# Fused attention and soft mixture of experts: the second expert layer of the last four experts by column halves

## The chip, the cores and the metric

The kernel runs on one core of a Trainium2 chip, as one program. The metric is the device time of one execution in microseconds. A core has the engines TensorE (PE; its weight loads are listed as PEld), VectorE (DVE), ScalarE (ACT), GpSimd (POOL) and SyncE (SP), which issues nearly all DMA transfers here. Sixteen DMA engines move the data.

## The reference

Attention over q, k, v of 8 batches, 8 heads, 576 tokens and 64 elements a head keeps for each query only the keys whose score is within tau of the best. Its output, 4608 tokens by 512, is the input x of a soft mixture of 8 experts with 4 slots each:

```python
logits = x @ phi                                   # 4608 x 32
d = softmax(logits, axis=0); slot_input = d.T @ x  # 32 slots x 512
for e in range(8):                                 # 4 slots per expert
    h = np.maximum(slot_input[e] @ w1[e], 0.0)     # 512 -> 1024
    slot_out[e] = h @ w2[e]                        # 1024 -> 512
c = softmax(logits, axis=1)
out = c @ slot_out                                 # 4608 x 512, fp32
```

## The kernel before

Attention, the logits and the running slot inputs take the first 469 us; a planner's table orders their instructions. The change touches only what follows. There each engine runs its instructions in the order in which the code names them, and so do the transfers on SyncE's queue.

The weights come in 32 units of 1 MiB: 0 to 15 are w1, 16 to 31 are w2, numbered by group of four experts (`a` is 0 or 1), by half of the contracted axis (`K`) and by expert in the group (`g`). So units 24 to 27 are the first half of w2 of experts 4 to 7, and 28 to 31 (`LAST`) the second. A unit is a tile of 128 partitions by 2048 elements; for w2 it holds 4 rows (`j`) of 512 columns in each partition. Units 0 to 22 and half of unit 31 (`early`, its rows j = 2, 3) are loaded during attention, the others when the first layer (`stage1`) frees a tile. `load_unit` loads each of the units 28 to 31 in two parts: first rows j = 0, 1 of all four, then rows j = 2, 3 of units 28 to 30, with 4 KB in one piece from each partition. That is seven transfers of 512 KB.

The second layer (`stage2`) multiplies `hz`, the transposed hidden values masked by expert, with w2. Four experts run side by side in four groups of 32 rows of TensorE, and all steps but the last add into one PSUM bank `so`. The last step (rows j = 2, 3 of units 28 to 31) goes into two other banks `end`, one for each half of the 512 columns, and meanwhile ScalarE copies `so` to SBUF (L1706). `combine` adds the banks to that copy (L1648), sums the four groups with a matmul by `st4` (L1651), and makes `sh` of it (L1652, L1653), which holds each value as two parts for the faster matmul type float32r.

The output of batch b is `cT` of the batch (128 by 512) times `sh`: four matmuls of 128 tokens, each 512 columns wide, into four PSUM banks (L1671). ScalarE copies two of them to SBUF (L1673), VectorE two (L1675), and SyncE writes them (L1679), 1 MiB for a whole batch with 8 KB in one piece per partition. Batch 0 goes in jobs of 1, 1 and 2 of its four parts, batch 1 in jobs of 2 and 2; the first job is done by column halves (L1664). A ninth batch holds the 64 last tokens of all eight batches (L1681). `ct` makes the next batch's `cT`: GpSimd scales the coefficients, TensorE transposes them (L976), ScalarE casts (L1570), VectorE subtracts (L1571). It is called after each batch, and there are three `cT` buffers.

Of the kernel before, what the change touches and what calls it, by code (L numbers as in the profile page):

```python
# [10 lines left out]
F32 = mybir.dt.float32  # L11
F32R = mybir.dt.float32r
# [826 lines left out]
def softmax_attention_soft_moe(  # L839
# [17 lines left out]
    nc = tc.nc  # L857
# [84 lines left out]
    wslots = [wp.tile([128, 2048], F32, name=f"w{i}") for i in range(NPRE)]  # L942
    where = {}
    early = wp.tile([128, 2, 512], F32, name="early")

    def load_early():
        e, K = units[-1][1:]
# [2 lines left out]
    def load_unit(t):  # L950

        i = len(where)
        if i == n_units:
            return
        where[i] = t
        kind, e, K = units[i]
        if kind == 0:
            nc.sync.dma_start(t.rearrange("p (j f) -> p j f", j=2),
                              w1[e, K * 256:(K + 1) * 256, :].rearrange("(j p) f -> p j f", j=2))
            return  # L960
        src = lambda e: w2[e, K * 512:(K + 1) * 512, :].rearrange("(p j) f -> p j f", j=4)
        if i not in LAST:
            nc.sync.dma_start(t.rearrange("p (j f) -> p j f", j=4), src(e))
        for k, h in [(i, 0)] * (i in LAST) + [(k, 1) for k in LAST[:-1]] * (i == LAST[-1]):
            nc.sync.dma_start(where[k].rearrange("p (j f) -> p j f", j=4)[:, 2 * h:2 * h + 2],
                              src(units[k][1])[:, 2 * h:2 * h + 2])


    rows = [slice(0, 64), slice(64, 128)]
# [532 lines left out]
    order_all.enter_context(tc.manual_schedule())  # L1502
    ps_h = ctx.enter_context(tc.tile_pool(name="ps_h", bufs=1, space=PSUM, reuse_waits="tile"))
    ps_t = ctx.enter_context(tc.tile_pool(name="ps_t", bufs=3, space=PSUM, reuse_waits="tile"))
    st4 = tl.tile([128, 4, 32], F32, name="st4")
    for g in range(4):
        nc.gpsimd.tensor_copy(st4[:, g, :], st1)
    neg = tl.tile([128, 1], F32, name="neg")
    for g in range(4):
        nc.gpsimd.memset(neg[g * 32:(g + 1) * 32], -1.0 if g % 2 else 0.0)  # L1510
# [5 lines left out]
    def ttile(name):  # L1516
        return ps_t.tile([128, 512], F32, tag="t", name=name)
# [22 lines left out]
    def ct():  # L1540


        if len(cTs) == len(blocks):
            return
        while len(c4s) < min(len(cTs) + 2, len(blocks)):
            c4s.append(c_block(*blocks[len(c4s)]))
        k = blocks[len(cTs)][1]
        c4 = c4s[len(cTs)]
        n = 128 * k
        t = tl.tile([128, SM], F32R, tag="cT", name=f"cT{len(cTs)}", bufs=3)  # L1550
        if len(cTs) < 2:
            w = two(f"ct{len(cTs)}", "h00" if cTs else "h01")
            for i in range(k):
                split(w, i, c4[:, i].rearrange("p g s -> p (g s)"))
            tv = t.rearrange("p (i g q) -> p i g q", i=4, g=2)
            for g in range(2):
                wv = w[g][:, 0:256].rearrange("p (i q) -> p i q", i=4)
                nc.scalar.copy(tv[:, :, g], wv)
                nc.vector.tensor_tensor(
                    out=tv[64:128, :, g], in0=wv[64:128], in1=tv[64:128, :, g].bitcast(F32), op=ALU.subtract)  # L1560
            cTs.append(t)
            return
        w = ttile(f"ct{len(cTs)}")
        for i in range(k):
            tr(w[:, i * 128:(i + 1) * 128], c4[:, i].rearrange("p g s -> p (g s)"))
        tv, wv = t[:, 0:n], w[:, 0:n]
        if len(cTs) == B:
            tv = t.rearrange("p (c r b) -> p b r c", c=4, b=B)
            wv = w.rearrange("p (b r c) -> p b r c", c=4, b=B)
        nc.scalar.copy(tv, wv)  # L1570
        nc.vector.tensor_tensor(out=tv[64:128], in0=wv[64:128], in1=tv[64:128].bitcast(F32), op=ALU.subtract)  # L1571
        cTs.append(t)
# [29 lines left out]
                    op=ALU.mult,  # L1602
                )

    def stage2(a, K, h):
        w = range(n_units // 2 + (a * 2 + K) * 4, n_units // 2 + (a * 2 + K) * 4 + 4)
        t = [where[i].rearrange("p (j f) -> p j f", j=4) for i in w]

        if a == NG - 1 and K == 1 and h == 1:
            for n, g in enumerate((3, 0, 1, 2)):  # L1610
                for q, dst in enumerate(end):
                    x = slice(q * DM // 2, (q + 1) * DM // 2)
                    for j in (2, 3):
                        m = (n + q) % 2 * 2 + j - 2
                        nc.tensor.matmul(
                            dst[m * 32:(m + 1) * 32, 0:DM // 2], hz[a][:, K * 4 + j, g * 32:(g + 1) * 32],
                            t[g][:, j, x] if g < 3 else early[:, j - 2, x], start=n < 2, stop=n > 1,
                            tile_position=(0, 32 * m), skip_group_check=True)
            return
        for j in (2 * h, 2 * h + 1):  # L1620
            for g in range(4):
                nc.tensor.matmul(
                    so[g * 32:(g + 1) * 32, :], hz[a][:, K * 4 + j, g * 32:(g + 1) * 32], t[g][:, j],
                    start=(a, K, j) == (0, 0, 0), stop=(a, K, j) == (NG - 1, 1, 1),
                    tile_position=(0, 32 * g), skip_group_check=True)
        if h:
            for i in w:
                load_unit(where[i])

    cnt = [-1]  # L1630

    def otile(name):
        cnt[0] += 1
        k = cnt[0] % 6
        return ps_h.tile([128, 512], F32, tag=("h01", "h10", "h11")[k // 2], name=name) if k % 2 else ttile(name)

    def through():

# [2 lines left out]
            last[id(where[i])] = (i, where[i])  # L1641
        return [t for i, t in sorted(last.values(), key=lambda x: x[0])]

    def combine():

        cols = [slice(n * DM // 2, (n + 1) * DM // 2) for n in range(2)]
        for q, w in zip(cols, end):
            nc.vector.tensor_tensor(out=so_sb[:, q], in0=w[:, 0:DM // 2], in1=so_sb[:, q], op=ALU.add)  # L1648
        for q, x in enumerate(cols):
            w = ttile(f"sr{q}")  # L1650
            nc.tensor.matmul(w[:, 0:DM // 2], st4.rearrange("p g s -> p (g s)"), so_sb[:, x], start=True, stop=True)  # L1651
            nc.scalar.copy(sh[:, x], w[:, 0:DM // 2])  # L1652
            nc.vector.scalar_tensor_tensor(  # L1653
                out=sh[:, x], in0=sh[:, x].bitcast(F32), scalar=neg, in1=w[:, 0:DM // 2], op0=ALU.mult, op1=ALU.add)
        free = through()

        jobs = [(0, 0, 1), (0, 1, 1), (0, 2, 2), (1, 0, 2), (1, 2, 2)] + [(b, 0, 4) for b in range(2, B + 1)]
        for n, (b, k, z) in enumerate(jobs):
            ot = free[b].rearrange("p (c d) -> p c d", c=4)[:, k:k + z]
            token = lambda c: slice(k + c, SM, 4) if b < B else slice(c * 128, c * 128 + 128)  # L1660
            for q, x in enumerate(cols if n == 0 else []):
                for c in range(z):
                    w = otile(f"o{n}_{c}_{q}")[:, 0:DM // 2]
                    nc.tensor.matmul(w, cTs[b][:, token(c)], sh[:, x], start=True, stop=True)  # L1664
                    if q:
                        nc.vector.tensor_copy(ot[:, c, x], w)
                    else:
                        nc.scalar.copy(ot[:, c, x], w)
            ws = [otile(f"o{n}_{c}") for c in range(z if n else 0)]
            for c in range(len(ws)):  # L1670
                nc.tensor.matmul(ws[c], cTs[b][:, token(c)], sh, start=True, stop=True)  # L1671
                if c % 2 == 0:
                    nc.scalar.copy(ot[:, c], ws[c])  # L1673
                else:
                    nc.vector.tensor_copy(ot[:, c], ws[c])  # L1675
            if k + z == 4:
                ct()
            if b < B:
                nc.sync.dma_start(out[b * S:b * S + SM].rearrange("(p c) d -> p c d", c=4)[:, k:k + z], ot)  # L1679
            else:  # L1680
                nc.sync.dma_start(out.rearrange("(b s) d -> b s d", s=S)[:, SM:S].rearrange(  # L1681
                    "b (r c) d -> r b (c d)", c=4), ot.rearrange("p c d -> p (c d)"))

    hp = [[ps_h.tile([128, 512], F32, tag=f"h{a}{n}", name=f"h{a}_{n}") for n in range(2)] for a in range(NG)]
    hid = [where[0][:, a * F:(a + 1) * F] for a in range(NG)]
# [4 lines left out]
    for a in range(NG):  # L1690
        for K in range(2):
            stage1(a, K, hp[a])
            if a == 0 and K == 0:
                for _, _, fn in csoft(slice(row(B - 1), NR)):
                    fn()
            if a and K == 0:
                hidden(a - 1)
        relu(a, hp[a])
    ct()
    ct()  # L1700
    end[:] = [ps_h.tile([128, 512], F32, tag=t, name=t + "e") for t in ("h00", "h11")]
    for a in range(NG):
        for K in range(2):
            for h in range(2):
                if a == NG - 1 and K == 1 and h == 1:
                    nc.scalar.copy(so_sb, so)  # L1706
                stage2(a, K, h)
            if a < NG - 1 and K == 0:
                hidden(a + 1)
    combine()  # L1710
    order_all.close()


# [45 lines left out]
```

## Time and profile before

| | us |
|---|---|
| runs, median of 3 (lowest to highest) | 535.15 (534.55 to 535.35) |
| span of the profiled execution, first to last instruction | 533.2 |
| first matmul of the first expert layer (L1579) | 468.85 |
| first instruction that waited for the last weights | 500.97 |
| issue of the first output transfer | 505.32 |
| issue of the last output transfer | 523.83 |

For the profiled execution no time is given but its span; the median is 1.95 us longer. Over the span TensorE is busy 97%, VectorE 88%, ScalarE 84%; 83.26 MB were moved, of which 9.44 MB are output. The stretch that the change touches is the last 50 us, so it has to be read by windows and by the timeline there, not from the shares of the whole span.

### The profile page before, as it was taken

Reading aid. Unit: us, or ns where it says so; the run is one execution under the profiler, and the core shown is the slowest. Engines: PE = TensorE matmul, PEld = TensorE weight load, DVE = VectorE, ACT = ScalarE, POOL = GpSimd, SP = SyncE. Lnnn points to the kernel's source line nnn. Section 1 sums busy time; section 2 is a strip of 40 time slices with the busy share of each in tenths; the row PEclk is TensorE's granted clock in tenths of the full one; section 3 lists DMA queues with packets and bytes.
Section 4 is the critical chain, followed back from the end, with each engine's and each line's share of the span. In section 5 each row is a group of like instructions: output and inputs, shape, how many; then the busy total and the mean of one; then the engine's idle time right before and its main releaser. Section 6 shows DMA issues by size and latency. Waiting matters only on the chain.

```text
span 533.2 us, 21792 instructions
## 1 busy us (share of the span) xinstructions
PE 514.7 (97%) x8877; PEld 403.5 (76%) x8877; DVE 467.3 (88%) x1311; ACT 447.4 (84%) x750; POOL 247.6 (46%) x444
## 2 busy tenths in 40 slices
PE   8999999999999999999999999999999999999881
PEld 5877888888878888888788888888788877643470
DVE  6999998999899998999899989999999999613282
ACT  3899998999899989998999989999899899612271
POOL 2475554556446454655356635554464546021030
PEclk9999999999999999999999999999999999999996
DMA  6333335333337314732953355353466315999398
GB/s 157 94 93 94 93 98 172 96 94 93 94 99 245 93 35 100 256 78 67 284 140 96 92 172 173 94 133 94 104 225 188 83 20 176 368 401 389 158 399 301
DMA packets 28868, 83.26 MB, mean 156 GB/s; under 512 B 4064, under 2 KB 12256, under 8 KB 26336
## 3 DMA queue, kind: packets, MB, share of 16 engines
q1 hardware_dynamic: 28448, 81.43, 49.5%
q8 instruction: 70, 1.15, 0.9%
q10 hardware_dynamic: 320, 0.44, 0.3%
q14 instruction: 30, 0.25, 0.2%
HBM read 72.42 MB, written 9.44 MB: 154 GB/s over the span
## 4 chain that ended last, share of the span: by engine, by line
PE 86%; DMA 4%; ACT 3%; DVE 3%; issue 2%; SPq 0%; DVEq 0%; ACTq 0%
PE ps L1068 24%; PE ps L1211 22%; PE ps L984 19%; PE ps L1234 4%; PE ps L1223 4%; PE ps L1073 3%; DMA w<-in_w 3%; PE ps L1268 2%; PE h L1579 2%; PE ps L1326 2%; PE ps L1376 2%; PE ps L1178 1%; ACT cT L1570 1%; DVE cT L1571 1%; PE ct L976 1%
## 5 line engine op out<-in xcount | busy, mean ns | idle before, releaser
L1080 DVE TENSOR_SCALAR_CACHE_REDUCE ss<-ps 128x576 f32<-128x576 f32 x288 | 208.3, 751 | 4.6 <-PE ps L1068 1.4
L1096 DVE SCALAR_TENSOR_TENSOR p<-ss,thr,p 128x576 f32<-128x576 f32 x256 | 203.6, 821 | 3.8 <-POOL thr L1093 1.6
L1093 POOL TENSOR_SCALAR thr<-nmx,pabs 128x1 f32<-128x1 f32 x288 | 136.1, 480 | 146.5 <-DVE ss L1080 143.2
L1090 ACT ACTIVATE p<-ss,nmx 128x576 f32<-128x576 f32 x256 | 188.6, 781 | 12.6 <-DVE ss L1080 11.6
L1068 PE MATMUL ps<-k,q 64*128 64x288 f32 x1024 | 154.9, 423 | 0.4
L1068 PEld LDWEIGHTS ps<-k,q 64*128 64x128 f32 x1024 | 87.5, 188 | 23.6 <-ACT pTa L989 5.1
L984 PEld LDWEIGHTS ps<-ident,p 64*128 64x128 f32 x2304 | 91.8, 138 | 17.2 <-DVE ss L1080 2.3
L984 PE MATMUL ps<-ident,p 64*128 64x64 f32 x2304 | 101.4, 223 | 0.2
L989 ACT COPY pTb<-ps 128x1024 f32<-128x1024 f32 (+1 forms) x96 | 83.8, 877 | 2.1 <-PE ps L984 0.7
L989 ACT COPY pTa<-ps 128x1024 f32<-128x1024 f32 x64 | 65.1, 1017 | 0.4 <-PE ps L984 0.2
L1211 PE MATMUL ps<-pTa,vv 128*64 128x128 f32 x992 | 61.0, 276 | 0.1
L1211 PE MATMUL ps<-pTb,vv 128*64 128x128 f32 x992 | 60.4, 274 | 0.0
L1211 PEld LDWEIGHTS ps<-pTa,vv 128*64 128x64 f32 x992 | 53.5, 137 | 5.5 <-issue 4.3
L1211 PEld LDWEIGHTS ps<-pTb,vv 128*64 128x64 f32 x992 | 53.6, 137 | 3.3 <-issue 2.8
L1263 POOL TENSOR_TENSOR x<-x,ri 128x512 f32<-128x512 f32 x31 | 37.2, 1201 | 10.3 <-ACT x L989 10.3
L1122 POOL TENSOR_SCALAR pL<-pL,ri 128x576 f32<-128x576 f32 x31 | 26.0, 840 | 15.2 <-DVE ri L1121 14.2
L1048 POOL TENSOR_SCALAR k<-k,flag 128x576 f32<-128x576 f32 x31 | 31.7, 1023 | 0.8 <-DMA k<-in_kT 0.4
L989 ACT COPY pTl<-ps 128x256 f32<-128x256 f32 x64 | 27.5, 429 | 3.3 <-PE ps L984 2.9
L1119 POOL TENSOR_SCALAR ri<-r 128x9 f32<-128x9 f32 x31 | 7.1, 229 | 45.4 <-DVE p L1096 44.6
L1223 PE MATMUL ps<-pTl,vv 64*64 64x128 f32 x496 | 26.5, 284 | 0.5 <-DVE ss L1080 0.5
L1249 ACT COPY xT<-ps 128x256 f32<-128x256 f32 x62 | 23.2, 374 | 4.4 <-PE ps L1211 2.6
L1532 POOL TENSOR_TENSOR w<-lall,crow 128x512 f32<-128x512 f32 x9 | 9.3, 1046 | 37.7 <-PE ct L976 24.4
(175 smaller groups left out, 609.0 us busy)
## 6 DMA issues: line engine op xcount, KB each, us to landing
w<-in_w SPq DMA_DIRECT2D x18, 1024.0 KB, 8.2
q<-in_qT SPq DMA_DIRECT2D x62, 288.0 KB, 4.5
vv<-in_vt SPq DMA_DIRECT2D x32, 320.0 KB, 4.8
host<-in_w SPq DMA_DIRECT2D x10, 1024.0 KB, 8.2
k<-in_kT SPq DMA_DIRECT2D x62, 144.0 KB, 4.2
out<-host SPq DMA_DIRECT2D x7, 1024.0 KB, 6.9
w<-in_w SPq DMA_DIRECT2D x7, 512.0 KB, 14.4
out<-host SPq DMA_DIRECT2D x2, 512.0 KB, 3.0
```

Of the source, the lines that this page charges most:

```text
L984: nc.tensor.transpose(out=s[:, g, c:c + 64], in_=ins[g], identity=ident[rows[g], rows[g]], tile_position=(64 * g, 0))
L989: G.add("ACT", 51 + 0.833 * n, nom, lambda: nc.scalar.copy(*io()), r, w)
L1048: sc = lambda e, kc=kc: lambda: e.tensor_scalar(out=kt.t[:, kc], in0=kt.t[:, kc], scalar1=flag8, **one)
L1068: nc.tensor.matmul(s.t[:, g, 0:HS], qt.t[rows[g], h, c * 128:(c + 1) * 128], kt.t[rows[g], h * HS:(h + 1) * HS], start=True, stop=True, ti ...
L1080: dve(678, t + OFF['mx'], [s], [ss, nmx], lambda s=s, ss=ss, nmx=nmx: nc.vector.tensor_scalar(out=ss.t.rearrange("p (a k) -> p a k", a=2), ...
L1090: G.add("ACT", 674, t + OFF['ex'], lambda sv=sv, nmx=nmx, view=view: nc.scalar.activation(view().rearrange("p (a k) -> p a k", a=2), sv(), ...
L1093: pool(250, t + OFF['th'], pre=75, fn=lambda nmx=nmx, thr=thr: nc.gpsimd.tensor_scalar(out=thr.t, in0=nmx.t, scalar1=1.0, scalar2=pabs, op ...
L1096: fn=lambda sv=sv, thr=thr, view=view, i=i: nc.vector.scalar_tensor_tensor(out=view().rearrange("p (a k) -> p a k", a=2), in0=sv(), scalar ...
L1122: pool(725, t + OFF['sc'], lambda: nc.gpsimd.tensor_scalar(out=pL.t[:, SL:SL + S], in0=pL.t[:, SL:SL + S], scalar1=ri.t[:, 8:9], **one), [ ...
L1211: nc.tensor.matmul(area(w, h, l)[rows[a]], vv.t[:, (h * 4 + kb) * 64:][:, 0:64], pT.t[:, h, kb, a * 128:(a + 1) * 128], tile_position=(0, ...
L1223: nc.tensor.matmul(area(ab[l], h, l)[rows[a]], vv.t[rows[h], SM + h * 64:][:, 0:64], pTl.t[rows[h], (l * 2 + a) * 128:][:, 0:128], tile_po ...
L1263: G.add("POOL", 1040, u + 6.8, own=f"new{j}" + group(b), r=[ri], w=[x[j]], fn=lambda: nc.gpsimd.tensor_tensor(out=wide(), in0=wide(), in1= ...
```

## The change

`load_unit` loads units 28 to 31 by column halves: columns 0 to 255 of all four rows j of units 28 to 30 and of rows 0, 1 of unit 31, then columns 256 to 511 of the same. That is eight transfers (six of 512 KB, two of 256 KB), in pieces of 1 KB.

The bank `so` now holds experts 0 to 3 alone. For experts 4 to 7 the whole second layer goes into the two banks `end`: `half(q, j)` multiplies one row j of units 24 to 27 for column half q, `half_unit(q, g)` all four rows of one of the units 28 to 31. `total(q)` does for one column half what the beginning of `combine` did for both. `out_half(b, q)` makes one column half of a batch's output: four matmuls of 256 columns into two banks, one copy each on ScalarE and VectorE, and one transfer of 512 KB in pieces of 1 KB. `out_whole(b)` is the old job for a whole batch.

The order is: column half 0 of experts 4 to 7, its total between the steps of half 1, then for each of the units 28 to 31 its second half followed by the output of column half 0 of batch 0, 1, 2 or 3 (and `ct` after the first two), then the total of half 1, the second column halves of batches 0 to 3 with a `ct` after each, and the other batches whole. `st4` moves from a tile of its own into the tile of unit 2, and `cT` gets a fourth buffer.

```diff
+    cols = [slice(n * DM // 2, (n + 1) * DM // 2) for n in range(2)]
...
-        for k, h in [(i, 0)] * (i in LAST) + [(k, 1) for k in LAST[:-1]] * (i == LAST[-1]):
-            nc.sync.dma_start(where[k].rearrange("p (j f) -> p j f", j=4)[:, 2 * h:2 * h + 2],
-                              src(units[k][1])[:, 2 * h:2 * h + 2])
+        for k, q in [(i, 0)] * (i in LAST) + [(k, 1) for k in LAST] * (i == LAST[-1]):
+            js = slice(0, 2 if k == LAST[-1] else 4)
+            nc.sync.dma_start(where[k].rearrange("p (j f) -> p j f", j=4)[:, js, cols[q]], src(units[k][1])[:, js, cols[q]])
...
-    st4 = tl.tile([128, 4, 32], F32, name="st4")
-    for g in range(4):
-        nc.gpsimd.tensor_copy(st4[:, g, :], st1)
...
-        t = tl.tile([128, SM], F32R, tag="cT", name=f"cT{len(cTs)}", bufs=3)
+        t = tl.tile([128, SM], F32R, tag="cT", name=f"cT{len(cTs)}", bufs=4)
...
+    def product(a, K, j, g, m, w, dst, q, **kw):
+        nc.tensor.matmul(dst[m * 32:(m + 1) * 32, 0:q.stop - q.start], hz[a][:, K * 4 + j, g * 32:(g + 1) * 32], w[:, q],
+                         tile_position=(0, 32 * m), skip_group_check=True, **kw)
+
+    def stage2(a, K):
+        t = w2_units(a, K)
+        for j in range(4):
             for g in range(4):
...
+                product(a, K, j, g, g, t[g][:, j], so, slice(0, DM), start=(K, j) == (0, 0), stop=(K, j) == (1, 3))
+
+    def half(q, j):
+
+        t = w2_units(NG - 1, 0)
+        for g in range(4):
+            product(NG - 1, 0, j, g, g, t[g][:, j], end[q], cols[q], start=j == 0, stop=False)
+
+    def half_unit(q, g):
+
+        t = w2_units(NG - 1, 1)[g]
+        for j in (2, 3, 0, 1):
+            w = early[:, j - 2] if g == 3 and j > 1 else t[:, j]
+            product(NG - 1, 1, j, g, j, w, end[q], cols[q], start=False, stop=g == 3)
+
+    def total(q):
+
+        x = cols[q]
+        nc.vector.tensor_tensor(out=so_sb[:, x], in0=end[q][:, 0:DM // 2], in1=so_sb[:, x], op=ALU.add)
+        w = ttile(f"sr{q}")
+        nc.tensor.matmul(w[:, 0:DM // 2], st4.rearrange("p g s -> p (g s)"), so_sb[:, x], start=True, stop=True)
+        nc.scalar.copy(sh[:, x], w[:, 0:DM // 2])
+        nc.vector.scalar_tensor_tensor(
+            out=sh[:, x], in0=sh[:, x].bitcast(F32), scalar=neg, in1=w[:, 0:DM // 2], op0=ALU.mult, op1=ALU.add)
...
+        return ps_h.tile([128, 512], F32, tag=("h01", "h10", "so")[k // 2], name=name) if k % 2 else ttile(name)
...
+    def out_half(b, q):
+
+        ot = through()[b].rearrange("p (c d) -> p c d", c=4)[:, :, cols[q]]
+        for k in range(2):
+            w = otile(f"o{b}_{q}_{k}").rearrange("p (c d) -> p c d", c=2)
+            for c in range(2):
+                nc.tensor.matmul(w[:, c], cTs[b][:, token(b, 2 * k + c)], sh[:, cols[q]], start=True, stop=True,
+                                 skip_group_check=True)
+            if k:
+                nc.vector.tensor_copy(ot[:, 2 * k:2 * k + 2], w)
             else:
...
+                nc.scalar.copy(ot[:, 2 * k:2 * k + 2], w)
+        nc.sync.dma_start(out[b * S:b * S + SM].rearrange("(p c) d -> p c d", c=4)[:, :, cols[q]], ot)
...
+    st4 = where[2][:, 3 * DM:3 * DM + 128].rearrange("p (g s) -> p g s", g=4)
+    for g in range(4):
+        nc.gpsimd.tensor_copy(st4[:, g, :], st1)
...
-    for a in range(NG):
-        for K in range(2):
-            for h in range(2):
-                if a == NG - 1 and K == 1 and h == 1:
-                    nc.scalar.copy(so_sb, so)
-                stage2(a, K, h)
-            if a < NG - 1 and K == 0:
-                hidden(a + 1)
-    combine()
+    for K in range(2):
+        stage2(0, K)
+        if K == 0:
+            hidden(1)
+    nc.scalar.copy(so_sb, so)
+    for j in range(4):
+        half(0, j)
+    for g in range(4):
+        half_unit(0, g)
+    for j in range(4):
+        half(1, j)
+        if j == 1:
+            total(0)
+    for g in range(4):
+        half_unit(1, g)
+        out_half(g, 0)
+        if g < 2:
+            ct()
+    total(1)
+    for b in range(4):
+        out_half(b, 1)
+        ct()
+    for b in range(4, B + 1):
+        out_whole(b)
```

## Rows read from the trace of the kernel before

**Rows 1.** Windows, us: busy PE, PEld, DVE, ACT, POOL; clock, DMA share, GB/s:
```profile
490.00:495.00 5.00, 5.00 (x52) 1.55 (x46) 0.00 (x0) 0.00 (x0) 0.00 (x0) 1.00 1.00 397
...
497.00:498.00 1.00, 0.83 (x9) 0.29 (x12) 0.00 (x0) 0.00 (x0) 0.00 (x0) 1.00 0.61 246
...
499.00:500.00 1.00, 1.00 (x17) 0.58 (x15) 0.00 (x0) 0.59 (x1) 0.00 (x0) 1.00 0.10 41
500.00:501.00 1.00, 0.47 (x13) 0.03 (x5) 0.00 (x0) 0.00 (x0) 0.00 (x0) 1.00 0.03 12
...
505.00:506.00 1.00, 1.00 (x8) 0.93 (x8) 0.61 (x2) 0.82 (x2) 0.00 (x0) 1.00 0.00 0
506.00:507.00 1.00, 1.00 (x5) 0.79 (x4) 0.56 (x2) 1.00 (x3) 0.81 (x1) 1.00 0.82 309
...
527.00:528.00 1.00, 0.00 (x0) 0.00 (x0) 0.00 (x0) 0.00 (x0) 0.00 (x0) 0.50 1.02 262
...
530.00:531.00 1.00, 0.00 (x0) 0.00 (x0) 0.00 (x0) 0.00 (x0) 0.00 (x0) 0.50 0.71 254
```

**Rows 2.** Timeline, 479 to 519 us (start, length, instruction, idle before it):
```profile
479.60 8.89 SPq L965 DMA_DIRECT2D w<-in_w  x7
...
497.23 0.16 PEld L1622 LDWEIGHTS so<-w,w 128*32 128x32 f32 x8 [1.07 <-DMA w<-in_w]
...
499.72 0.11 PEld L1615 LDWEIGHTS h00e<-w,w 128*32 128x32 f32 x2 [0.20 <-DMA w<-in_w]
...
500.97 0.11 PEld L1615 LDWEIGHTS h00e<-w,w 128*32 128x32 f32 x2 [1.01 <-DMA w<-in_w]
...
501.21 0.39 PE L1615 MATMUL h00e<-w,w 128*32 128x256 f32 x2
...
501.70 0.42 DVE L1648 TENSOR_TENSOR w<-h00e,w 128x256 f32<-128x256 f32 x1 [11.99 <-issue]
...
502.18 1.13 PE L1651 MATMUL sr<-w,st 128*128 128x256 f32 x4 [0.57 <-DVE w L1648]
...
503.94 0.85 PE L1664 MATMUL o<-sh,cT 128*128 128x256 f32 x2 [0.64 <-DVE sh L1653]
...
505.32 1.42 SPq L1679 DMA_DIRECT2D out<-w  x3
...
507.62 0.63 PE L976 MATMUL ct<-ident,w 128*128 128x128 f32 x4 [0.52 <-DVE cT L1571]
...
508.00 1.46 PE L1671 MATMUL o<-sh,cT 128*128 128x512 f32 x4
...
518.91 1.16 ACT L1570 CAST cT<-ct 128x512 fp32r<-128x512 f32 x1 [0.56 <-PE ct L976]
```

**Rows 3.** DMA view, 516 to 520 us, 8 KB output packets:
```profile
DMA packets 233, 1.65 MB, mean 414 GB/s; under 512 B 31, under 2 KB 31, under 8 KB 31
```

**Rows 4.** DMA view, 492 to 497 us, 4 KB weight packets:
```profile
DMA packets 565, 2.05 MB, mean 410 GB/s; under 512 B 64, under 2 KB 64, under 8 KB 565
```

**Rows 5.** DMA view, 506.2 to 506.8 us, 2 KB output packets:
```profile
DMA packets 110, 0.23 MB, mean 375 GB/s; under 512 B 0, under 2 KB 0, under 8 KB 110
```

**Rows 6.** DMA view, 258.8 to 259.2 us, 1152 B key packets:
```profile
DMA packets 127, 0.13 MB, mean 330 GB/s; under 512 B 15, under 2 KB 126, under 8 KB 127
```

**Rows 7.** Groups by line and shape, 478 to 533 us (busy us, mean ns, idle):
```profile
L1675 DVE COPY host<-o 128x512 f32<-128x512 f32 x16 | 10.2, 686 | 0.2
...
L1673 ACT COPY host<-o 128x512 f32<-128x512 f32 x16 | 8.7, 604 | 0.8 <-PE o L1671 0.8
...
L1571 DVE TENSOR_TENSOR cT<-ct,cT 64x512 fp32r<-64x512 f32 x7 | 5.3, 756 | 1.7 <-ACT cT L1570 1.1
L1570 ACT CAST cT<-ct 128x512 fp32r<-128x512 f32 x7 | 4.7, 673 | 3.4 <-PE ct L976 3.4
```

**Rows 8.** SyncE's issues of key loads and outputs, ns min/median/max:
```profile
L1032 SPq DMA_DIRECT2D k<-in_kT x62: 595/616/1390, 6.1 to 422.2; - x62
...
L1679 SPq DMA_DIRECT2D out<-host x8: 332/332/333, 508.3 to 522.6; - x8
```

More of the change, by code (lines that the diff above doesn't have):

```diff
@@ L1603, in hidden, with w2_units @@
                 )
-    def stage2(a, K, h):
+    def w2_units(a, K):
         w = range(n_units // 2 + (a * 2 + K) * 4, n_units // 2 + (a * 2 + K) * 4 + 4)
-        t = [where[i].rearrange("p (j f) -> p j f", j=4) for i in w]
-        if a == NG - 1 and K == 1 and h == 1:
[L1610 to L1620, printed above, removed]
-            for g in range(4):
[L1622 to L1628, printed above, removed]
@@ new lines, in w2_units @@
+        return [where[i].rearrange("p (j f) -> p j f", j=4) for i in w]
+    def product(a, K, j, g, m, w, dst, q, **kw):
[4 more added lines that the diff above has]
+        for j in range(4):
+            for g in range(4):
+                product(a, K, j, g, g, t[g][:, j], so, slice(0, DM), start=(K, j) == (0, 0), stop=(K, j) == (1, 3))
@@ L1634, in otile @@
         k = cnt[0] % 6
-        return ps_h.tile([128, 512], F32, tag=("h01", "h10", "h11")[k // 2], name=name) if k % 2 else ttile(name)
+        return ps_h.tile([128, 512], F32, tag=("h01", "h10", "so")[k // 2], name=name) if k % 2 else ttile(name)
     def through():
@@ L1642, in through @@
         return [t for i, t in sorted(last.values(), key=lambda x: x[0])]
[L1644 to L1679, printed above, removed]
-            else:
-                nc.sync.dma_start(out.rearrange("(b s) d -> b s d", s=S)[:, SM:S].rearrange(
-                    "b (r c) d -> r b (c d)", c=4), ot.rearrange("p c d -> p (c d)"))
@@ new lines, in token @@
+    def token(b, c):
+        return slice(c, SM, 4) if b < B else slice(c * 128, c * 128 + 128)
+    def out_half(b, q):
[7 more added lines that the diff above has]
+                nc.vector.tensor_copy(ot[:, 2 * k:2 * k + 2], w)
+            else:
+                nc.scalar.copy(ot[:, 2 * k:2 * k + 2], w)
+        nc.sync.dma_start(out[b * S:b * S + SM].rearrange("(p c) d -> p c d", c=4)[:, :, cols[q]], ot)
@@ new lines, in out_whole @@
+    def out_whole(b):
+        ot = through()[b].rearrange("p (c d) -> p c d", c=4)
+        ws = [otile(f"o{b}_{c}") for c in range(4)]
+        for c in range(4):
+            nc.tensor.matmul(ws[c], cTs[b][:, token(b, c)], sh, start=True, stop=True)
+            if c % 2 == 0:
+                nc.scalar.copy(ot[:, c], ws[c])
+            else:
+                nc.vector.tensor_copy(ot[:, c], ws[c])
+        ct()
+        if b < B:
+            nc.sync.dma_start(out[b * S:b * S + SM].rearrange("(p c) d -> p c d", c=4), ot)
+        else:
+            nc.sync.dma_start(out.rearrange("(b s) d -> b s d", s=S)[:, SM:S].rearrange(
+                "b (r c) d -> r b (c d)", c=4), ot.rearrange("p c d -> p (c d)"))
@@ L1701, in softmax_attention_soft_moe @@
     end[:] = [ps_h.tile([128, 512], F32, tag=t, name=t + "e") for t in ("h00", "h11")]
-    for a in range(NG):
-        for K in range(2):
-            for h in range(2):
-                if a == NG - 1 and K == 1 and h == 1:
-                    nc.scalar.copy(so_sb, so)
-                stage2(a, K, h)
-            if a < NG - 1 and K == 0:
-                hidden(a + 1)
-    combine()
+    for K in range(2):
[19 more added lines that the diff above has]
+        out_half(b, 1)
+        ct()
+    for b in range(4, B + 1):
+        out_whole(b)
     order_all.close()
```

## Prediction

> **What bounds the kernel now.** I read the windows first, then the timeline of the tail, then the DMA packets by size, then the durations of the few instructions that the change rearranges. Everything before 490 us is the same in both kernels, so the argument is about the last 43 us. In that stretch the DMA engines are the bound, and they are idle once. Their share is 1.00 while the last w2 units come in, falls from 497 on (0.61, then 0.10: most of the 16 engines are done and a few lag), is about zero from 500, and is 0.82 again in the microsecond from 506 [rows 1]. So the engines stand still for about 6 us, and partly for 3 us more. After that they are full until the last 1 MiB, which is slow (262 GB/s at 527) and ends near 531.1 [rows 1]. What fills the hole is one chain: the last weights release TensorE at 500.97, VectorE adds from 501.70, the sum over the expert groups starts at 502.18, the first output matmul at 503.94, and SyncE issues the first output transfer at 505.32 [rows 2]; its packets run from about 506.2, some 0.85 us after the issue. That output stream then sets the end. I check it: 16 packets of 2 KB per engine, 24 of 4 KB and 48 of 8 KB, at the prices below, are 1.4 + 3.8 + 15.2 = 20.4 us, so 526.6, and the slow last transfer takes 4.5 us more: 531.1, as the share is falling (0.71 from 530).
>
> **The price of a packet.** With the engines full the rate gives the time of one packet on one engine (16 times its size over the rate): 8 KB at 414 GB/s is 317 ns, 4 KB at 410 is 160, 2 KB at 375 is 87, and the 1152 B packets of the key loads at 330 are 56 [rows 3 to 6]. The change makes 1 KB packets, which no row shows. From below, the line through 8 and 4 KB gives 42 ns; from above, the 1152 B packets in proportion and the line through 4 and 2 KB give 50 and 51. I take 48, and keep 42 and the whole 56 as ends.
>
> The Trainium skill (DMA: Bandwidth & Descriptors, Specifications) puts the smallest transfer that still runs at line rate at 512 B. By that a 1 KB packet would cost an eighth of an 8 KB one, some 40 ns; the trace disagrees, since its packets of 1152 B reach 330 GB/s where 8 KB reach 414.
>
> **The change, part by part.**
>
> *Loads.* The same 3.5 MiB of units 28 to 31 come as 1 KB runs instead of 4 KB runs. The releases by weights stand 1.25 us apart on the latest engine (499.72 to 500.97), so the seven old transfers begin there at about 500.97 - 7 x 1.25 = 492.2 [rows 2]. The first column halves are 3 x 32 + 16 = 112 packets per engine, 5.4 us: they are all there at 497.6. The second halves take as long again: the first unit's lands at 499.1, the last's at 503.0, 2 us later than now.
>
> *First half.* After 497.6 TensorE does the last unit's half. Two rounds of four 256-column matmuls start 0.24 us apart [rows 2], so a unit is some 0.43 us and one step of the K=0 product as much. With the two steps that stand ahead of it, the group sum starts at 497.6 + 3 x 0.43 + 0.05 = 498.95; from there to the first output matmul the old chain took 503.94 - 502.18 = 1.76, so 500.7. The other two steps and the first unit of the second half fit beside it (498.95 + 0.43 + 0.86 + 0.43 = 500.67; its weights are there at 499.1). Four 512-column output matmuls take 1.46 us, the last ending 0.47 after its start, so they stand 0.33 apart [rows 2]; at 256 columns it can be half of that if the columns bind, or the same if the weights' load does. I take 0.22: the fourth result is there 1.15 us after the first start, and TensorE is busy for 0.9. VectorE's copy takes 0.69 [rows 7]. Issue at 502.55. The three-dimensional pattern costs SyncE 0.62 instead of 0.33 (the key loads, which have such a pattern, against the outputs) [rows 8], so I count 1.1 to the first packet: 503.65. The writing thus begins 2.5 us earlier than now.
>
> *Cadence.* Ahead of the next half batch TensorE has 0.9 for the output, 0.45 for the four transposes of a coefficient block (0.63 with the drain of the last [rows 2]) and 0.43 for a unit: 1.78. VectorE has a copy and a subtraction, 0.69 + 0.76, ScalarE less [rows 7]: TensorE sets the pace. The third half batch is issued at 506.1, the fourth, without a block, at 507.45. One write is 32 x 48 = 1.54 us: 503.65 to 505.2, 505.45 to 507.0, 507.2 to 508.75, 508.75 to 510.3.
>
> *Second half.* Its add stands behind the fourth half batch's copy on VectorE, and with it everything after: 507.4 + 0.42 + 0.05 + 1.76 = 509.65, then 1.15 + 0.69 to the issue at 511.5, and 1.1 to the packet: 512.6. So 2.3 us of idle DMA come back at 510.3. This wait is what replaces the one that is removed.
>
> *Rest.* From 512.6 the queue stays fed: 4 x 1.54 = 6.15 for second halves, 4 x 2.53 = 10.1 for whole batches, 4.5 for the remainder, and 0.3 for the last coefficient block, whose 1.16 us cast [rows 2] now comes between batches 4 and 5: 533.65. The last write ended at 531.1, so the span grows by 2.55 us. The profiled span is 533.2; the median of the three runs, 535.15, has 1.95 us outside it, which the change leaves alone. Forecast: 537.7 us.
>
> *At nothing:* the group-sum matrix moved into a weight tile (GpSimd copies it long before 498, behind nothing that waits); the fourth coefficient buffer; the earlier copy of the accumulator on ScalarE, which has nothing to do between 490 and 495 [rows 1]; the added weight loads of TensorE, which run beside the matmuls of a stretch where TensorE ends up waiting for the weights' transfer (1.07 us before 497.23 [rows 2]); without that wait they would lengthen it. The one more load on SyncE stands among issues that are over at 488.5 (479.60 + 8.89 [rows 2]), far ahead of the first output's at 502.55.
>
> So the balance is: the second half's first packet must start by 531.1 - 21.05 = 510.05 for no change. The ends of the matmul spacing (0.16, where VectorE paces the half batches, to 0.33) move 512.6 to about 511.5 and 514.4; the ends of the packet price move the loads' landing by -0.7 and +0.9 and the writes behind by -0.8 and +1.0.
>
> **Rivals.** (1) *Dear packets*: they cost 56 ns or more, as the key loads' do. Landing moves 0.9 us, the last four half writes 1.0, and each half write becomes longer than the cadence, which only shortens the idle: 539.6, or more if half rows slow the memory. For it speaks the nearest row; against it that those loads cover half the partitions. (2) *No second hole*: the add and the sum hide behind the first-half writes, because TensorE and VectorE go faster through the half batches than I count. The output then runs without a gap from 503.65: 8 x 1.54 + 10.1 + 4.5 = 26.9, 530.6, so 534.7: not slower. It decides at the 510.3 where the first halves' writes end: the hole has to close by all of its 2.3 us. Against it speaks that the chain of 2.23 from add to output matmul and then 2.9 to the packet is made of durations in the rows. (3) *Free packets* with the hole left: 39.6 ns each. Landing is 0.95 earlier, the hole is then at 509 to 511.65, four half writes take 5.1 and the rest 14.9: 531.65, so 535.7, no change. The rows of 2 KB and 1152 B speak against it. The Trainium skill's line rate from 512 B (DMA: Bandwidth & Descriptors, Specifications) is this rival's rule. (4) *Both 2 and 3*: writing from 502.7 without a gap, 10.1 + 10.1 + 4.5: 527.4, so 531.4, faster.
>
> **Numbers.** Chances: forecast 0.50, with its own range 536.6 to 539.3; dear packets 0.13; no second hole 0.15; free packets 0.10; both 0.12. Within 0.2% (1.1 us, about what the runs can tell) lie cases 2 and 3, 0.25; faster 0.12; slower 0.63. The range leaves out case 4 and the worst of case 1: 534.2 to 540.2.
>
> **What would show it.** In the windows after: a share near 1 to about 499, a first hole of about 4 us that ends near 503.7, a second one around 510 to 512.6, and no third. In the timeline the first output issue near 502.5 and the fifth near 511.5, with VectorE's second add directly behind the fourth half batch's copy. Packets of 1 KB at about 340 GB/s where the engines are full. I am wrong if the fifth write starts by 510, or if 1 KB packets run at 400 GB/s or under 300.

## The result, and the profile after

The changed kernel takes 540.12 us in the median of 4 runs (538.71 to 542.59), the kernel before 534.86 beside it (534.55 to 535.35): a ratio of 1.0102, 95% interval 1.0074 to 1.0130. Slower was forecast, and the time lies within the range, but the loss is 5.3 us where the forecast had 2.55. A repeat of both (in the experiments) gives 6.0.

The profiled execution has a span of 537.8 us (before: 533.2). The windows of the tail answer to [rows 1] (same columns: busy PE, PEld, DVE, ACT, POOL; granted clock, DMA share, GB/s):

```profile
498.00:499.00 1.00, 1.00 (x21) 0.40 (x10) 0.42 (x1) 0.00 (x0) 0.00 (x0) 1.00 1.11 350
...
501.00:502.00 1.00, 1.00 (x8) 0.92 (x4) 0.00 (x0) 0.14 (x1) 0.00 (x0) 1.00 0.10 35
...
503.00:504.00 1.00, 1.00 (x11) 0.77 (x4) 0.64 (x2) 0.36 (x1) 0.93 (x1) 1.00 0.00 0
504.00:505.00 1.00, 1.00 (x10) 0.81 (x14) 0.59 (x2) 0.66 (x2) 0.00 (x0) 1.00 0.61 212
...
506.00:507.00 1.00, 1.00 (x11) 0.55 (x10) 0.60 (x2) 0.59 (x1) 0.08 (x1) 1.00 0.49 172
...
508.00:509.00 1.00, 0.30 (x2) 0.10 (x1) 0.66 (x1) 0.46 (x1) 0.00 (x0) 1.00 0.43 149
509.00:510.00 1.00, 0.37 (x2) 0.30 (x2) 0.46 (x2) 0.00 (x0) 0.00 (x0) 1.00 1.01 341
510.00:511.00 1.00, 0.30 (x2) 0.00 (x0) 0.25 (x1) 0.37 (x1) 0.00 (x0) 1.00 0.82 282
...
513.00:514.00 1.00, 1.00 (x7) 1.00 (x6) 0.33 (x2) 0.73 (x2) 0.62 (x1) 0.50 0.00 0
514.00:515.00 1.00, 1.00 (x6) 1.00 (x5) 0.97 (x2) 0.34 (x1) 0.42 (x1) 0.50 0.51 176
...
535.00:536.00 1.00, 0.00 (x0) 0.00 (x0) 0.00 (x0) 0.00 (x0) 0.00 (x0) 0.50 0.80 270
```

The DMA column tells the story. The first hole is there and shorter than before (some 3 us, from 501.5 to 504.4). Then come dips at 506 and 508, where each half write is over before the packets of the next begin. The second hole, forecast from 510.3 to 512.6, stands from 512 to 514.5. The last write ends near 536.0, where it was 531.1.

The timeline of the same stretch (start, length, instruction, idle before it; weight loads and other lines between are left out) answers to [rows 2]:

```profile
496.94 0.64 PE L1608 MATMUL h00e<-w,w 128*32 128x256 f32 x8 [0.96 <-DMA w<-in_w]
...
498.33 0.42 DVE L1633 TENSOR_TENSOR w<-h00e,w 128x256 f32<-128x256 f32 x1 [7.93 <-issue]
499.02 0.70 PE L1635 MATMUL sr<-w 128*128 128x256 f32 x2
...
501.08 1.21 PE L1663 MATMUL o<-sh,cT 128*128 128x256 f32 x4
502.13 0.60 PE L977 MATMUL ct<-ident,w 128*128 128x128 f32 x4
502.33 0.69 DVE L1666 COPY w<-o 128x512 f32<-128x512 f32 x1 [1.69 <-PE o L1663]
502.66 0.64 PE L1608 MATMUL h11e<-w,w 128*32 128x256 f32 x8
503.09 0.62 SPq L1669 DMA_DIRECT2D out<-w  x1
503.23 1.02 PEld L1663 LDWEIGHTS o<-sh,cT 128*128 128x128 f32 x4 [0.41 <-issue]
505.25 4.38 SPq L1669 DMA_DIRECT2D out<-host  x3
...
508.34 0.69 DVE L1666 COPY host<-o 128x512 f32<-128x512 f32 x1 [1.01 <-PE o L1663]
509.06 0.42 DVE L1633 TENSOR_TENSOR w<-h11e,w 128x256 f32<-128x256 f32 x1
509.63 0.67 PE L1635 MATMUL sr<-w 128*128 128x256 f32 x2 [1.33 <-DVE w L1633]
...
511.28 1.21 PE L1663 MATMUL o<-sh,cT 128*128 128x256 f32 x4 [0.98 <-DVE sh L1637]
...
513.28 0.53 SPq L1669 DMA_DIRECT2D out<-w  x1
513.94 1.05 PE L977 MATMUL ct<-ident,w 128*128 128x128 f32 x4
```

Two things can be read. First, the mechanism: VectorE's second add (509.06) has no idle time ahead of it, because it stands directly behind the fourth half batch's copy (508.34 + 0.69); from there sum, copy, output and issue follow one another to 513.28, and the DMA engines run dry meanwhile. Second, the pace: from one round of output matmuls to the next TensorE needs 1.05 (501.08 to 502.13), 0.53 and 0.57 us, 2.15 in all.

The packets: the first DMA line is the loads from 492 to 499, the second the half writes from 517 to 518; they answer to [rows 3 to 6].

```profile
DMA packets 2471, 2.45 MB, mean 350 GB/s; under 512 B 82, under 2 KB 2471, under 8 KB 2471
...
DMA packets 336, 0.34 MB, mean 344 GB/s; under 512 B 0, under 2 KB 336, under 8 KB 336
```

At 344 GB/s with a share of 1.01 a 1 KB packet takes 16 x 1024 / 344 = 47.6 ns; the loads, with several transfers queued at once, show a mean of 50 ns for one packet. The forecast had 48.

### The profile page after: what moved, and what is told of

It reads as the page before. It is cut to its first block, busy times and chain, and to the rows that moved or that the text cites. A ratio compares the mean times of both kernels' runs of the same rounds, so it can differ in the third digit from the quotient of the medians.

```text
span 537.8 us, 21917 instructions
## 1 busy us (share of the span) xinstructions
PE 518.2 (96%) x8940; PEld 409.6 (76%) x8940; DVE 468.3 (87%) x1311; ACT 448.0 (83%) x749; POOL 246.8 (46%) x444
## 4 chain that ended last, share of the span: by engine, by line
PE 90%; DMA 3%; ACT 2%; DVE 2%; issue 1%; DVEq 0%; POOL 0%; POOLq 0%; ACTq 0%
PE ps L1069 25%; PE ps L1212 22%; PE ps L985 19%; PE ps L1235 4%; PE ps L1224 4%; PE ps L1074 4%; DMA w<-in_w 3%; PE h L1577 2%; PE ps L1269 2%; PE ps L1327 2%; PE ps L1377 2%; PE o L1663 2%; PE ps L977 1%; PE ps L1179 1%; PE h11e L1608 1%
## 5 line engine op out<-in xcount | busy, mean ns | idle before, releaser
L1097 DVE SCALAR_TENSOR_TENSOR pL<-ss,thr,pL 128x576 f32<-128x576 f32 x32 | 26.1, 814 | 0.3
```

Of the source, the lines that this page charges most:

```text
L1097: fn=lambda sv=sv, thr=thr, view=view, i=i: nc.vector.scalar_tensor_tensor(out=view().rearrange("p (a k) -> p a k", a=2), in0=sv(), scalar ...
```

## The experiments

Every ratio is against the kernel before, run beside it on the same chip. The end of the last write is read from the DMA share of the last microseconds.

| kernel | median us (runs) | ratio, 95% interval | end of the last write, us |
|---|---|---|---|
| the change | 540.12 (4) | 1.0102, 1.0074 to 1.0130 | 536.0 |
| e9_after, the change repeated | 540.35 (5) | 1.0109, 1.0094 to 1.0124 | 537.0 |
| e10_busy | 538.41 (6) | 1.0077, 1.0063 to 1.0091 | 536.0 |
| e2_blocks | 538.00 (6) | 1.0072, 1.0051 to 1.0092 | 534.3 |
| e3_loads | 537.51 (11) | 1.0049, 1.0036 to 1.0063 | 534.0 |
| e4_writes | 537.16 (6) | 1.0047, 1.0029 to 1.0066 | 532.5 |
| e1_total | 537.06 (9) | 1.0052, 1.0032 to 1.0071 | 534.2 |
| e5_both | 535.93 (12) | 1.0025, 1.0012 to 1.0039 | 533.4 |
| e6_order | 535.32 (12) | 1.0011, 0.9999 to 1.0023 | 531.2 |
| e7_two | 534.45 (12) | 0.9999, 0.9989 to 1.0010 | 530.5 |
| e8_before, before repeated | 534.96 (8) | 1.0003, 0.9989 to 1.0018 | 531.4 |

**e1_total: the second sum is moved ahead of the fourth half batch.** The add no longer stands behind that batch's copy.

```diff
     for g in range(4):
         half_unit(1, g)
+        if g == 3:
+            total(1)
         out_half(g, 0)
         if g < 2:
             ct()
-    total(1)
```

> The changed kernel with one thing moved: the second half's add and group sum stand directly behind the last unit's matmuls, ahead of the fourth half batch's output. Theory of the second hole (the add waits behind that output's copy on VectorE, and the DMA engines stand idle from 512.0 to about 514.4 for it): the add starts near 507.4 instead of 509.06, the fifth output issue comes about 1.8 us earlier than 513.28, and the time falls by 1.5 to 2 us, to about 538.3. Rival theory of the packets (the loss is the price of the 1 KB packets and of what they do to the memory, and the hole only takes up slack): no change from 540.1, within 0.5 us.

Measured: 1.0052, half of the loss gone. From the first issue to the fifth 8.49 us pass, where the change has 10.19; so the add's place gives 1.7 us, as expected, and the median fell by more (some 2.7). In the windows the second hole has shrunk from 2.4 us to some 1.2:

```profile
507.00:508.00 1.00, 0.34 (x2) 0.31 (x3) 0.58 (x2) 0.00 (x0) 0.00 (x0) 1.00 0.87 296
...
509.00:510.00 1.00, 0.86 (x4) 0.67 (x4) 0.94 (x2) 0.36 (x1) 0.00 (x0) 1.00 0.96 328
510.00:511.00 1.00, 1.00 (x6) 1.00 (x6) 0.34 (x1) 0.58 (x1) 0.00 (x0) 0.68 0.01 1
511.00:512.00 1.00, 1.00 (x7) 1.00 (x5) 0.35 (x1) 0.48 (x2) 0.37 (x1) 0.50 0.79 273
```

The chain behind the fourth copy is thus a cause of the loss, and the price of the packets (unchanged here) isn't all of it.

**e2_blocks: the two coefficient blocks leave the loop of first halves.** They are formed ahead of the last units, where TensorE waits for weights anyway.

```diff
         half(0, j)
+    ct()
+    ct()
     for g in range(4):
         half_unit(0, g)
...
         out_half(g, 0)
-        if g < 2:
-            ct()
```

> The changed kernel with one thing moved: the coefficient blocks of batches 2 and 3 are made before experts 4 to 7, where TensorE ends up waiting for weights, and not between the first half batches. Theory of TensorE's pace (half batches come every 2.15 us and not every 1.78, since a block and two changes between 32-column and 128-column matmuls stand between them): the three issues after the first come about 1.7 us apart, the fifth about 0.9 us earlier, and the time falls by about 0.9 us, to 539.2. Rival theory of the packets: no change from 540.1.

Measured: 1.0072. SyncE's part of the timeline:

```profile
502.26 0.62 SPq L1669 DMA_DIRECT2D out<-w  x1
503.96 3.95 SPq L1669 DMA_DIRECT2D out<-host  x3
511.54 0.53 SPq L1669 DMA_DIRECT2D out<-w  x1
```

The first halves are now issued 1.70 us apart, and the second half's first write at 511.54 in place of 513.28, 9.28 us behind the first issue: 0.9 less than in the change, as expected, while the median fell by some 1.6. The hole itself stays (share 0.11, 0.00 and 0.23 in the microseconds from 510, 511 and 512): pace and hole are two separate costs.

**e5_both: the two edits together.**

> Both moves at once: the second half's add and sum directly behind the last unit, and the coefficient blocks of batches 2 and 3 made early. If the lost time is a chain on TensorE and VectorE that sets when the second halves can be written, the two gains add until the first halves' writes (6 us from about 503.5) set the time: fifth issue near 510, no idle DMA of more than about 1 us there, 1.0 to 1.8 us over the kernel before. If the packets are the loss and the hole only slack, it is no better than the better of the two alone, 2.6 us over before.

Measured: 1.0025. Each edit keeps its worth beside the other: the fifth issue comes 7.48 us after the first (the change 10.19, e1_total 8.49, e2_blocks 9.28). The clock is 1.00 in every microsecond of the tail up to 520, where e1_total and e2_blocks have 0.50 from 511 to 513. Yet TensorE was busy here much as in e1_total in the microseconds before (0.36 at 507 here, 0.34 there, and 0.86 at 509 in both). So which idle time brings the clock down isn't shown by these two.

**e3_loads: only the loads and the accumulation by column halves**; both sums come at the end, and the output is written as before the change.

```diff
         half(1, j)
-        if j == 1:
-            total(0)
     for g in range(4):
         half_unit(1, g)
-        out_half(g, 0)
-        if g < 2:
-            ct()
+    total(0)
     total(1)
-    for b in range(4):
-        out_half(b, 1)
-        ct()
-    for b in range(4, B + 1):
-        out_whole(b)
+    old_jobs()
```

(`old_jobs` is the output loop of the kernel before; `cT` has three buffers again.)

> Only the loads and the accumulation by column halves; the sums of both halves come together at the end and the output is written as in the kernel before, in pieces of 2, 4 and 8 KB. Price of the loads by the packets' measured 50 ns: 224 x 50 = 11.2 us against 56 x 160 = 9.0, so the last weights release TensorE 2.0 to 2.2 us later and, as nothing is hidden, the time is that of before and 2.2 us: 537.1. If the loads were free it would be 534.9; by the rival of packets that are dear beyond their own time, 538.5 or more.

Measured: 1.0049, some 2.6 us, but not by the way that was expected. The last weights release TensorE at 501.70, where it was 500.97 [rows 2] and, in a second profile of the kernel before (e8_before), 501.58: 0.1 to 0.7 us later, not 2.0 to 2.2. From that release to the first issue 5.95 us pass, where both profiles before have 4.35:

```profile
501.70 0.64 PE L1608 MATMUL h11e<-w,w 128*32 128x256 f32 x8 [0.69 <-DMA w<-in_w]
...
504.07 0.48 DVE L1637 SCALAR_TENSOR_TENSOR sh<-sh,neg,sr 128x256 fp32r<-128x256 f32 x1 [5.44 <-ACT sh L1636]
504.46 0.42 DVE L1633 TENSOR_TENSOR w<-h11e,w 128x256 f32<-128x256 f32 x1
...
504.94 0.70 PE L1635 MATMUL sr<-w 128*128 128x256 f32 x2 [1.31 <-DVE w L1633]
...
507.65 1.76 SPq L1682 DMA_DIRECT2D out<-w  x3
```

The second half's add (504.46) stands directly behind the first half's subtraction (504.07) on VectorE; `combine` made both adds first. Behind it the granted clock falls, and the DMA share falls once more:

```profile
509.00:510.00 1.00, 1.00 (x4) 0.82 (x4) 0.22 (x2) 0.82 (x2) 0.71 (x1) 0.50 1.04 393
...
511.00:512.00 1.00, 1.00 (x7) 0.99 (x5) 0.81 (x3) 0.67 (x3) 0.52 (x1) 1.00 0.19 74
```

From the first issue to the end of the last write 26.4 us pass, in place of 25.8 and 25.4. So most of the 2.6 us belongs to the order of this experiment's own sums, and it is no price of the loads; what their 1 KB pieces cost by themselves isn't shown beyond the 0.1 to 0.7 us of the release.

**e4_writes: only the output by column halves**; the loads and the sums are those of the kernel before.

```diff
-        jobs = [(0, 0, 1), (0, 1, 1), (0, 2, 2), (1, 0, 2), (1, 2, 2)] + [(b, 0, 4) for b in range(2, B + 1)]
-        for n, (b, k, z) in enumerate(jobs):
...
+        for b in range(4):
+            for q in range(2):
+                out_half(b, q)
+            ct()
+        for b in range(4, B + 1):
+            out_whole(b)
```

> Only the writes: the kernel before, with its loads and sums, but batches 0 to 3 made and written by column halves, in pieces of 1 KB, after both sums. By the measured 47 ns: 256 x 47 = 12.1 us against 10.3, and a first issue about 0.5 us later than 505.32, since a half batch is larger than the old first job and its issue takes longer: before and 2.3 us, 537.2. If half rows slowed the memory beyond that, 538.5 or more; if the writes were free, about 535.4.

Measured: 1.0047, some 2.5 us, in the two parts that were expected: from the last weights' release (500.15) to the first issue (505.10) 4.95 us in place of 4.35, and from there to the end of the last write 27.4 in place of 25.8 and 25.4. The writes never wait for anything here; a full microsecond of them, and the end of the last:

```profile
512.00:513.00 1.00, 1.00 (x7) 0.99 (x8) 0.98 (x2) 0.68 (x2) 0.10 (x1) 1.00 1.00 348
...
532.00:533.00 1.00, 0.00 (x0) 0.00 (x0) 0.00 (x0) 0.00 (x0) 0.00 (x0) 0.50 0.50 188
```

The two losses together are about that of the change (2.6 and 2.5 against 5.3), but they aren't its two prices, since the first holds a wait of its own. What the overlap gave can be read in the changed kernel's windows: the writing begins at 504.4 in place of 506.2, 1.8 us earlier, and the second hole alone takes 2.5.

**e6_order: all that was learnt, in one order.** All K=0 steps of both column halves and two coefficient blocks go ahead of the last units; two first-half outputs are issued before the second halves' last units; the add of the second half stands before the third output, its sum before the fourth.

```diff
...
+    total(0)
+    group_sum(0)
+    half_unit(1, 0)
+    out_half(0, 0)
+    out_half(1, 0)
+    for g in range(1, 4):
         half_unit(1, g)
-        out_half(g, 0)
...
     total(1)
+    out_half(2, 0)
+    group_sum(1)
+    out_half(3, 0)
```

(`total` is now the add alone, `group_sum` the rest of it.)

> The changed kernel's work in the order that the chain theory calls for: experts 4 to 7's first half of the contracted axis for both column halves and two coefficient blocks while TensorE waits for weights, then the first total with one unit of the second half beside it, the outputs of two batches, the last three units, and the second total around the third batch's output. First issue about 1 us earlier than 503.1, fifth near 509, idle DMA of about 1 us in the middle. It still pays about 2.2 us for the loads in 1 KB pieces and 1.9 for the writes, so it should land within 0.7 us of the kernel before. By the packets' rival it stays 2 us or more over it.

Measured: 1.0011. The DMA engines work without a second hole from 504.4 on, but for a dip:

```profile
503.00:504.00 1.00, 1.00 (x18) 0.60 (x21) 0.74 (x2) 0.41 (x1) 0.00 (x0) 1.00 0.00 0
504.00:505.00 1.00, 1.00 (x18) 0.52 (x6) 0.25 (x1) 0.00 (x0) 0.00 (x0) 1.00 0.59 205
...
507.00:508.00 1.00, 0.85 (x4) 0.77 (x4) 0.81 (x2) 0.24 (x1) 0.00 (x0) 1.00 0.64 218
...
531.00:532.00 1.00, 0.00 (x0) 0.00 (x0) 0.00 (x0) 0.00 (x0) 0.00 (x0) 0.50 0.22 82
```

This is rival 2 made real. Its stream of 26.9 us, from 504.4, ends at 531.3, and in the trace it ends near 531.2: even with the hole closed, the writing's earlier start (1.8 us) is used up by the first four batches' writes, which take 12.3 us in 1 KB pieces (8 x 1.54) and 10.3 in the old ones.

**e7_two: half as many pieces.** In the order of e6_order only the last two units are loaded by column halves, and only batches 0 and 1 written so.

```diff
-    OWN, LAST = range(3), range(n_units - 4, n_units)
+    OWN, LAST = range(3), range(n_units - 2, n_units)
...
-    for b in range(4, B + 1):
+    for b in range(2, B + 1):
         out_whole(b)
```

> A cheaper form of the same: only units 30 and 31 come by column halves, 28 and 29 whole, and only batches 0 and 1 are written by halves, with the order of the experiment before. Half of the 1 KB pieces are gone (loads + 1.0 us, writes + 0.9 us), and less is hidden: the first issue near 504.8, the second total behind it without a hole. Expected within 0.7 us of the kernel before, with about as good a chance to be faster as slower.

Measured: 0.9999, no difference from before. No version that was tried beats the kernel before.

**e8_before: the kernel before, profiled again.**

> The kernel before once more, for a second profile: the first expert layer started at 468.9 us in the first one and at 469.2 to 470.0 in the profiles of the changed kernel and of the four experiments, though nothing ahead of it differs. If that is a difference from execution to execution, this one may start anywhere between; if the changed kernels start later because of what was changed, it starts at 468.9 again. From the first output transpose on, its tail should be 49.7 us as before, within 0.3.

Its first expert layer starts at 470.04 us, where it was 468.85, its first output is issued at 505.93, 0.6 us later than in [rows 2], and its span is 533.3. From the first output transpose on that is 48.6 us, not 49.7 within 0.3: part of the later start is made up. In the two profiles of the change the layer starts at 469.55 and 471.65. So a shift common to a whole tail isn't the change's doing, differences of a microsecond in the table's last column say little, and below I compare distances inside one execution.

**e9_after: the change, repeated.**

> The changed kernel itself, once more, since its four times spread over 3.9 us (538.71 to 542.59) where the other kernels spread over 1 to 4. If the excess over the forecast is what the profile shows (first packet of the second halves 1.9 us later than forecast, some 0.45 lost after it), the median should be about 533.65 + 2.35 + some 2.1 of the profile's stretch behind the last write + 1.8 outside the span = 539.9 at the most and 539 with the spread of the starts: 1.008 to 1.010 against before. If the change also makes the executions themselves uneven, the times spread over 4 us again and the median is 540 or more.

Measured: 540.35 (539.52 to 541.05), span 538.8. SyncE's timeline is that of the first profile about 1 us later:

```profile
504.05 0.62 SPq L1669 DMA_DIRECT2D out<-w  x1
506.20 4.39 SPq L1669 DMA_DIRECT2D out<-host  x3
514.34 0.53 SPq L1669 DMA_DIRECT2D out<-w  x1
```

The wide spread didn't come back (1.5 us in five runs); the loss, 6.0 us, is somewhat more than expected.

**e10_busy: TensorE is given work while the second sum is formed**: seven matmuls more, whose results nobody reads.

```diff
+    def busy(n):
+        for i in range(n):
+            nc.tensor.matmul(end[0][:, 0:DM // 2], cTs[0][:, token(0, 0)], sh[:, cols[0]], start=True, stop=True,
+                             skip_group_check=True)
...
         nc.tensor.matmul(w[:, 0:DM // 2], st4.rearrange("p g s -> p (g s)"), so_sb[:, x], start=True, stop=True)
+        if q:
+            busy(3)
...
+    busy(4)
     total(1)
```

> Seven matmuls of 256 columns are added, whose results nobody reads: four behind the fourth first-half output and three behind the second group sum, where TensorE otherwise waits (busy 0.30, 0.37, 0.30 in the microseconds from 508, 509, 510). Nothing that is computed changes. Theory A, that the granted clock's fall to 0.50 from 512.4 to 515.6 comes from this idle time and stretches the second halves: the clock stays at 1.00 there, the four second-half issues come 1.45 to 1.8 us apart in place of 2.09, 1.76, 1.45, and the time falls by 0.5 to 1.0 us against the changed kernel beside it, to some 1.007. Theory B, that the clock's fall is hidden behind the writes (each takes 1.54) or has another cause: the time stays within 0.3 us of the changed kernel beside it. In both the second hole stays, from 512 to 514.4.

Measured: 1.0077 against 1.0109 beside it, 540.35 to 538.41. The windows and one round of transposes, which took 1.05 us in the change (513.94):

```profile
510.00:511.00 1.00, 0.79 (x4) 0.79 (x5) 0.07 (x1) 0.08 (x1) 0.00 (x0) 1.00 0.78 269
...
513.00:514.00 1.00, 1.00 (x8) 1.00 (x7) 0.69 (x1) 0.67 (x2) 0.33 (x1) 1.00 0.00 0
514.00:515.00 1.00, 1.00 (x7) 0.98 (x8) 0.80 (x2) 0.69 (x3) 0.71 (x1) 1.00 0.00 0
```
```profile
514.30 0.60 PE L977 MATMUL ct<-ident,w 128*128 128x128 f32 x4
```

The clock stays at 1.00, and the hole stays as well (512.4 to 515.1): the fifth issue follows the first by 10.22 us, as in the change (10.19 and 10.29). That bears out theory A: the half clock was a cost of its own. Between the two profiles I find some 0.6 us of it, from the second halves' first packet to the end of the last write (21.5 in the repeat, 515.5 to 537.0, against 20.9 here, 515.1 to 536.0); the two profiles of the kernel before differ by 0.3 from their first packet to their last. The medians, whose runs spread over 1.5 and 1.8 us, differ by 1.9, more than the 0.5 to 1.0 expected. What the other 1.3 are is open.

## Why the prediction was half right

The direction and the mechanism were right; the step that failed is the cadence of the half batches, and with it the other terms that go by TensorE's pace: they were too small. By its own steps:

- *Packets*: 48 ns forecast, 47.6 and 50 measured. That rejects rival 1 (56 and more) and rival 3 (39.6). The Trainium skill's line rate from 512 B (DMA: Bandwidth & Descriptors, Specifications) isn't what this case shows: 1 KB packets ran at 344 to 350 GB/s, 8 KB at 414 [rows 3].
- *Loads*: the last first half was to land at 497.6; TensorE is released at 496.94, and at about 497.9 in the repeat. The last second half was to land at 503.0, 2 us later than before. In the changed kernel no instruction waits for it; in e3_loads, with the same loads, it releases TensorE at 501.70, so this term was too large, and nothing hung on it.
- *First half*: forecast from the group sum (498.95) to the issue (502.55): 3.60 us. Measured 499.02 to 503.09: 4.07. The 0.3 of it come ahead of the output matmuls (2.06 from the sum in place of 1.76): the matmuls of the second half that were to fit beside the sum hold TensorE from 499.65 to 501.15 (24 in the trace), where the forecast had it free at 500.67. Then 1.3 to the first packet in place of 1.1.
- *Cadence*, the term that failed most: 1.78 us forecast, 2.15 measured, with a block; 1.71 in place of 1.33 without one. Each of its three parts was too small: output 1.05 (forecast 0.9), transposes 0.53 (0.45), unit 0.57 (0.43). Two causes can be read: the output's weight loads take 1.02 us for four and the matmuls start no faster than these, and TensorE's loader is idle for 0.17 to 0.41 us at each change between matmuls on 32 columns of the array and on all 128 (the second layer's groups are of 32 columns, 128x32 in its weight loads, not of 32 rows, as the part on the kernel before has it), an item that the forecast lacked. Over three steps this makes 6.01 us in place of 4.9, so 1.1 too little. e2_blocks confirms what a block costs: 0.45 in each step that has one.
- *Second half*: the wait forecast, at its place. From the fourth issue to the fifth 4.18 us, forecast 4.05. Its first packet came at 514.5, forecast 512.6: the 1.9 us are 0.54 of the first issue, 1.1 of the cadence, 0.13 here and 0.14 of the packets' latency.
- *Rest*: forecast 21.05, measured 21.5, and 20.9 where the clock is kept up. The sum of the writes was thus right. What the forecast lacks is a term for the granted clock, at 0.50 from 513 to 515 behind 3 us in which TensorE was busy for a third.
- *Rival 2 and 4*: the hole didn't close; e6_order shows that closing it needs another order, and gives then the time of before, as rival 2 had it.
- *At nothing*: right, though one reason given was not. SyncE's issues of these loads take 15.60 us for eight in place of 8.89 for seven [rows 2], so they are over at 496.1, not 488.5; the first output's issue came 7 us later, so it cost nothing.

```profile
480.49 15.60 SPq L967 DMA_DIRECT2D w<-in_w  x8
```

In the profiled spans that adds up: 1.9 of the first packet and 0.45 of the rest on top of the 2.55 make 4.9, measured 4.6 (537.8 against 533.2). The medians show 0.7 to 1.4 us more than that. Some of it lies outside the span, which the forecast left alone: 1.93 to 3.0 us in the first four runs of the change and 1.75 to 2.05 in the repeat, against 1.76 to 1.91 in the kernel before beside it. The rest I can't place.

## What to carry to other kernels

Cutting transfers into smaller pieces so that writing can begin under the last loads has a price (here about 2 us of longer writing for 4 MiB in pieces of 1 KB); the gain exists only while the early writes last until the late ones are ready, so first work out whether the pipe runs dry a second time. In an order written by hand, an add that starts the last chain belongs ahead of copies whose writes can wait: moving one line gave back half of the loss. An experiment that takes out one part of a change also has an order of its own: read in its trace where its loss falls, before calling it that part's price. When several kinds of matmul alternate in a loop, take the pace from start to start in a trace with that alternation, not from the sum of the kinds.

## What the runs showed of the hardware

- TensorE's granted clock fell to half (1.2 in place of 2.4 GHz) in the microseconds 513 and 514 after TensorE had waited for most of the three from 508; with the seven added matmuls there (e10_busy) it stayed whole. In e1_total it fell from 510 on behind a single microsecond at 0.34 busy (507), in e5_both it stayed whole behind one at 0.36; why is open.
- The issues of the last loads took SyncE 15.60 us with 1 KB packets (eight transfers) and 8.89 with 4 KB (seven). Why they take longer isn't shown.
- With 1 KB packets the loads' last weights released TensorE only 0.1 to 0.7 us later (501.70 in e3_loads against 500.97 and 501.58), though by the time of the packets the loads take 2.2 us more (224 x 50 ns against 56 x 160).
- Writes of 1 KB pieces began 1.2 to 1.3 us after their issue, those of 2 KB rows before the change 0.85.
- At a change between matmuls on 32 columns and on 128 the weight loader stood idle for 0.17 to 0.41 us.
